# An MLP on one core: TensorE's instructions taken in the order of the program's text instead of the scheduler's

## The chip, the cores and the metric

The kernel runs on one core of a Trainium2 chip. The metric is the device time of one execution in microseconds (us); the median of several executions is compared. Engines are named as in the profile: PE (TensorE, matmuls), PEld (its weight loads), DVE (VectorE), ACT (ScalarE), POOL (GpSimd) and SP (SyncE, which here issues the DMAs).

## What is computed

One transformer block with adaptive layer norm, for 2048 tokens of width 576, in float32. Attention is linear; the MLP has 4608 hidden columns.

```python
mod = (_silu(c) @ w_mod).reshape(c.shape[0], 6, 1, -1)
sa, ca, ga, sb, cb, gb = (mod[:, i] for i in range(6))
h = _layernorm(x) * (1 + ca) + sa
x = x + ga * linear_attention(h, A_wqkv, A_wo)
h = _layernorm(x) * (1 + cb) + sb
x = x + gb * (_silu(h @ B_w1) @ B_w2)
```

## The kernel before

Every float32 product is made of rounded parts: an operand is split into a high part (a cast on ACT) and a low part (a subtraction, on DVE or POOL), and three matmuls (high by high, high by low, low by high) replace one.

The stages before the MLP (modulation, attention, the second layer norm, and the first of 18 groups of hidden columns) end at about 405 us. The change touches what follows: the MLP for groups 1 to 17, each of 256 hidden columns. A group is worked through in two **units**, one per pair of 512-token blocks, so there are 34 units. Both matrix products of the MLP are done by a Winograd scheme with seven products where eight block products would be needed:

- **Up** products (class Unit, `up`, matmuls at L941): seven per unit, taken in the order 1, 6, 2, 5, 7, 3, 4 (ORDER). Each has six matmuls of 128x512; products 2, 3, 4 and 5 have two more for the last 64 of the 576 columns (the tail). They accumulate in three of four PSUM banks named `up`. Between products DVE and ACT take results out: a copy to `p1` (L954), additions into four tiles `f` (L958, L965, L979) and SiLU (L961, L980). f of the first block's second half of columns is complete after product 3.
- **Operands** for the down products are made from the four `f` tiles by `operands1` and `operands2`: sums on POOL (L999 to L1010), casts on ACT (L989) and subtractions on DVE or POOL (L990), into the tiles ha, hd, hb, hc, he, one set for each block of the pair and one buffer for each tile.
- **Down** products (`down`, matmuls at L1029): fourteen per unit, numbered 0 to 13, seven for each block in the order ha, hd, hb, hb, hc, hc, he. Each has six matmuls of 128x288. They alternate between two PSUM buffers named `down`; after each product DVE adds the buffer into an accumulator in SBUF (L1033), and the product after the next one accumulates in the same buffer, so it waits for that addition. A unit's down products are done while the next unit's up products are done.
- **Streams**: ten of the fourteen up operands of a group don't fit in SBUF and are fetched from DRAM (`fetch`, L917), all seven of the first unit and three of the second. There are three rooms: when streamed product i is done, the fetch of product i+3 is issued. A fetch is 1024 KB, or 1280 KB with the tail.
- **Weights** (class Weights): the next group's weights are loaded (L871, L873, L889), summed on POOL (L862 to L865) and split by ACT and DVE (L883, L905, L62) while the present group runs.

In the last group the additions of U (L1047) and the stores of results come on top; after the last unit its first block has seven down products and its second block is done in plain form (`plain_down`, L1066, 48 matmuls).

The order of instructions on each engine is chosen by the scheduler, which works with a timeline of its own and, among instructions that are ready in it, takes the one that stands first in the program's text. Waits between engines are semaphores; each engine takes its instructions in the order chosen. In the text, the main loop (from L1085 on) writes for each of the seven up products of a unit: one down product of the unit before, the up product, one more down product:

```python
for q, n in enumerate(ORDER):
    if before:
        before.down(2 * q)
    unit.up(n)
    if before:
        before.down(2 * q + 1)
```

In the text below, d0 to d13 are down products and u1 to u7 up products by these numbers, a group is the two units of 256 hidden columns, and a unit takes 50 up matmuls and 84 down matmuls.

Of the kernel before, what the change touches and what calls it, by code (L numbers as in the profile page):

```python
# [21 lines left out]
def kernel(ctx: ExitStack, tc, A_x, A_wqkv, A_wo, B_x, B_w1, B_w2, c, w_mod, out):  # L22
# [8 lines left out]
    V, A, G, T = nc.vector, nc.scalar, nc.gpsimd, nc.tensor  # L31
# [16 lines left out]
    NG = F // (G2 * P)  # L48

    def f32(ap):  # L50
        return ap.bitcast(F32)
# [317 lines left out]
    def v_proj(t):  # L369
        ps, vt = ps2(), vx[t % 2]  # L370
        x_passes([(ps[:, 0, :NV0], cut(wkv, D, NV0)),
                  (ps[:, 1, : D - 2 * HG], cut(wkv, D + 2 * HG, D - 2 * HG))], xsel(t))
        for b, j, n, w in ((0, 0, 2, HG), (1, 2, 2, HG), (1, 4, 1, TAIL)):
            off = 2 * HG if j == 4 else 0
            src = ps[:, b, off : off + n * w].rearrange("p (n w) -> p n w", n=n)
            last = A.copy(vt[:, j : j + n, 0, :w], src), sub_hi(vt[:, j : j + n, 1, :w], src, vt[:, j : j + n, 0, :w])
        return last
# [38 lines left out]
    for t in range(NT):  # L416
        tb, i = t // 4, t % 4
        more = tb + 1 < NB
# [18 lines left out]
        before, after = after, v_proj(t)  # L437
# [8 lines left out]
        for _ in range((0, 2, 1, 1)[t] if t < 4 else 1):  # L446
            q = next(qs)
# [42 lines left out]
    for j, kv in enumerate(kvp):  # L490
        n = min(2, NHC - 2 * j)
# [90 lines left out]
    def load_mlp(g):  # L582
        f0 = g * FW
        r1 = rawp.tile([P, KC + 1, FW], F32, name="raw")
        nc.sync.dma_start(r1[:, 0:KC, :], B_w1[0 : KC * P, f0 : f0 + FW].rearrange("(k p) f -> p k f", p=P))
        for h in range(2):
            nc.sync.dma_start(r1[h * 64 : h * 64 + 64, KC, :], B_w1[KC * P : D, f0 : f0 + FW])
        w1 = wg.tile([P, 9, FW], F32R, name="w")
        A.copy(w1[:, 0:KC, :], r1[:, 0:KC, :])
        sub_hi(w1[:, KC : 2 * KC, :], r1[:, 0:KC, :], w1[:, 0:KC, :])  # L590
        wt = rawp.tile([P, 2, FW], F32R, name="wt")
        G.memset(f32(wt[64:128, 1, :]), 0.0)
        tail_w(wt, r1[:, KC, :])
        r2 = rawp.tile([P, KC + 1, FW], F32, name="raw").rearrange("p k f -> p (k f)")[:, : G2 * D]
        r2 = r2.rearrange("p (j d) -> p j d", j=G2)
        nc.sync.dma_start(r2, B_w2[f0 : f0 + FW, :].rearrange("(j p) d -> p j d", p=P))
        w2 = wg.tile([P, G2, 2, D], F32R, name="w")
        V.tensor_mul(r2, r2, bc["gb"].unsqueeze(1).to_broadcast([P, G2, D]))
        A.copy(w2[:, :, 0, :], r2)
        sub_hi(w2[:, :, 1, :], r2, w2[:, :, 0, :])  # L600
        return w1, w2, wt
# [75 lines left out]
    ORDER = (1, 6, 2, 5, 7, 3, 4)  # L677
# [101 lines left out]
    while s < NT + 5 or filler or turns:  # L779
        if s < QB - 2:  # L780
            filler.append(late_q)
        if s == 4:
            w = load_mlp(0)
# [4 lines left out]
        t = s - 2  # L788
# [36 lines left out]
    first = tc.alloc_tile_pool(name="first", bufs=1, reuse_waits="tile")  # L825
# [5 lines left out]
    U = [pf.tile([P, 2, HALF], F32, name=f"U{b}") for b in range(NB)]  # L831
# [80 lines left out]
    def fetch(i):  # L912
        if i < len(streamed):
            _, q, n = streamed[i]
            room = rooms0[i] if i < 2 else rooms[(i - 2) % 3]
            m = hd[q, n].shape[1]
            nc.sync.dma_start(f32(room[:, :m, :]), hd[q, n])  # L917
            in_room[i] = room
# [150 lines left out]
            V.tensor_add(halves(acc[t]), ps[:, :, :HALF], halves(acc[t]))  # L1069
            nc.sync.dma_start(of[t * P : (t + 1) * P, :], acc[t])  # L1070

    w = Weights(1)
    w.load1()
    w.sums1()
    for n in ORDER:
        w.up(n)
    w.load2()
    for i in range(5):
        fetch(i)
    for u in U:  # L1080
        G.memset(u, 0.0)
    ws = {1: w}
    ph, before = None, None
    units = [(g, p) for g in range(1, NG) for p in range(2)]
    for g, p in units:  # L1085
        unit = Unit(g, p, ws[g])
        more = g + 1 < NG
        if p == 1 and more:
            ws[g + 1] = Weights(g + 1)
            ws[g + 1].load1()  # L1090
            ws[g + 1].sums1()
        for q, n in enumerate(ORDER):
            if before:
                before.down(2 * q)
            unit.up(n)
            if before:
                before.down(2 * q + 1)
                if q == 0:
                    before.operands1(1)
                    before.operands2(1)  # L1100
            if p == 0 and q == 1:
                unit.w.sums2()
            if q == 2:
                if ph is None:
                    first.release()
                    ph = tc.alloc_tile_pool(name="ph", bufs=1, reuse_waits="tile")
                unit.operands1(0)
            if q == 5:
                unit.operands2(0)
            if p == 0:  # L1110
                unit.w.down(*{2: (1, 7), 4: (2, 4), 5: (5, 6), 6: (3,)}.get(q, ()))
            if p == 1 and more:
                ws[g + 1].up(n)
        if p == 1 and more:
            ws[g + 1].load2()
        before = unit
    unit.plain_operands(1)
    unit.add_u(3, (1, 1), (1, 0), (0, 1))
    for m in range(7):
        unit.down(m)  # L1120
    for t in range(4):
        unit.plain_down(1, t)
    psC.release()
    for p in (rs, ph, pf, wm, w2p, wqp, hTa, accp):
        p.release()
# [28 lines left out]
```

## Time and profile before

| | us |
|---|---|
| median of three runs | 1275.38 |
| lowest and highest | 1274.17, 1277.03 |
| the profiled execution | 1279.52 |
| its span (first to last instruction) | 1277.7 |
| first up matmul of the changed part | 405.31 |
| last matmul | 1273.64 |

Mean granted clock of TensorE over the span: 0.989.

| line, engine | what | count | busy, us | mean, ns |
|---|---|---|---|---|
| L1033 DVE | `acc` from a down product | 335 | 250.6 | 751 |
| L1033 DVE | `U` from a down product | 134 | 100.8 | 752 |
| L941 PE | up matmul, `hT` operand | 876 | 231.0 | 397 |
| L1029 PE | down matmul, `hc` operand | 804 | 128.2 | 300 |
| L980 ACT | SiLU | 102 | 64.4 | 631 |
| L990 POOL | subtraction for `hc` | 67 | 87.3 | 1303 |

How to read it: the page gives one profiled execution. Matmuls overlap in the pipeline, so a matmul's mean of 397 ns is longer than the step from one start to the next, and a busy share of PE near 1 doesn't mean that matmuls follow each other at full pace; the steps are read from the start times in the timeline. In brackets behind an instruction stand the idle time of its engine before it and what ended it.

### The profile page before, as it was taken

How to read it: one execution, taken by the hardware profiler on the slowest of the kernel's cores; microseconds unless marked ns; L12 is line 12 of the kernel's file. 1: busy time of each engine (PE TensorE's matmuls, PEld its weight loads, DVE VectorE, ACT ScalarE, POOL GpSimd, SP SyncE). 2: the span in 40 equal slices, each digit the busy share in tenths (PEclk: the TensorE clock that was granted, in tenths of full speed). 3: DMA queues.
4: the chain of work that ended last, by engine and by line, in shares of the span. 5: the costliest groups of instructions: out<-in, count | busy, mean ns of one | idle time of the engine just before them, and what ended most of it. 6: DMA issues, size and time to landing. Idle time of an engine off the chain costs nothing.

```text
span 1277.7 us, 19286 instructions
## 1 busy us (share of the span) xinstructions
PE 1190.5 (93%) x7167; PEld 1061.4 (83%) x7167; DVE 958.4 (75%) x1583; ACT 522.3 (41%) x1067; POOL 599.8 (47%) x673
## 2 busy tenths in 40 slices
PE   5999999999898899999999999999999999999997
PEld 4999999899786688888888888888788888888876
DVE  6655744988775688778788777787778777877877
ACT  5434332254553444434344344344344443443430
POOL 3200001322312577667476566665665665665641
PEclk9999999999898999999999999999999999999999
DMA  9221300213527877686576766865766777668623
GB/s 271 82 66 56 108 1 1 86 38 121 208 104 279 336 291 275 240 328 256 224 282 267 287 238 233 335 238 233 298 254 262 266 267 275 247 266 330 230 92 139
DMA packets 57579, 268.59 MB, mean 210 GB/s; under 512 B 5450, under 2 KB 20046, under 8 KB 34446
## 3 DMA queue, kind: packets, MB, share of 16 engines
q1 hardware_dynamic: 57486, 267.36, 55.8%
q8 instruction: 57, 0.93, 0.3%
q14 instruction: 36, 0.29, 0.1%
HBM read 250.56 MB, written 16.78 MB: 209 GB/s over the span
## 4 chain that ended last, share of the span: by engine, by line
PE 53%; DVE 19%; DMA 10%; issue 7%; POOL 7%; ACT 3%; SPq 0%; POOLq 0%; ACTq 0%; DVEq 0%
PE up L941 21%; PE down L1029 15%; PE psK L154 8%; DVE acc L1033 5%; DMA hT<-hd 5%; DVE w L62 4%; PE big L154 4%; DMA raw<-in_B_w_dram 2%; DVE hb L990 2%; PE big L655 1%; PE small L641 1%; DVE f L979 1%; POOL t L862 1%; POOL hc L990 1%; PE kvp L390 1%
## 5 line engine op out<-in xcount | busy, mean ns | idle before, releaser
L1033 DVE TENSOR_TENSOR acc<-down,acc 128x576 f32<-128x576 f32 x335 | 250.6, 751 | 86.7 <-PE down L1029 83.3
L941 PE MATMUL up<-hT,w 128*128 128x512 f32 x876 | 231.0, 397 | 14.0 <-DMA hT<-hd 10.2
L941 PEld LDWEIGHTS up<-hT,w 128*128 128x128 f32 x876 | 157.8, 188 | 47.6 <-ACT p L954 4.6
L1029 PE MATMUL down<-w,hc 128*128 128x288 f32 x804 | 128.2, 300 | 8.2 <-DVE acc L1033 6.9
L1029 PE MATMUL down<-w,hb 128*128 128x288 f32 x804 | 128.8, 300 | 7.2 <-DVE U L1033 4.6
L1029 PEld LDWEIGHTS down<-w,hc 128*128 128x128 f32 x804 | 115.9, 189 | 21.9 <-DVE acc L1033 13.8
L1029 PEld LDWEIGHTS down<-w,hb 128*128 128x128 f32 x804 | 117.5, 191 | 16.9 <-ACT ha L989 3.9
L154 PE MATMUL psK<-w,hT 128*128 128x288 f32 (+2 forms) x896 | 125.3, 297 | 3.0 <-DVE hT L62 1.1
L154 PEld LDWEIGHTS psK<-w,hT 128*128 128x128 f32 x896 | 120.8, 189 | 4.3 <-DVE hT L62 1.9
L1033 DVE TENSOR_TENSOR U<-down,U 128x576 f32<-128x576 f32 x134 | 100.8, 752 | 18.1 <-PE down L1029 16.3
L980 ACT ACTIVATE f<-f 128x512 f32<-128x512 f32 x102 | 64.4, 631 | 116.2 <-DVE f L979 114.3
L990 POOL TENSOR_TENSOR hc<-s,hc 128x512 fp32r<-128x512 f32 x67 | 87.3, 1303 | 31.8 <-ACT hc L989 31.3
L1005 POOL TENSOR_TENSOR s<-f,f 128x256 f32<-128x256 f32 x67 | 54.8, 819 | 94.0 <-ACT f L980 93.3
L941 PE MATMUL up<-room,w 128*128 128x512 f32 x336 | 89.8, 398 | 3.4 <-ACT w L883 2.8
L1010 POOL TENSOR_TENSOR f<-f,s 128x256 f32<-128x256 f32 x67 | 51.8, 773 | 83.2 <-DVE hb L990 81.7
L62 DVE TENSOR_TENSOR w<-raw,w 128x288 fp32r<-128x288 f32 (+2 forms) x139 | 76.3, 557 | 10.2 <-ACT w L883 7.6
L990 POOL TENSOR_TENSOR hd<-s,hd 128x256 fp32r<-128x256 f32 x67 | 54.2, 808 | 50.8 <-ACT hd L989 27.8
L1029 PE MATMUL down<-w,he 128*128 128x288 f32 x402 | 68.4, 305 | 8.4 <-DVE acc L1033 7.8
L941 PEld LDWEIGHTS up<-room,w 128*128 128x128 f32 x336 | 61.4, 190 | 15.6 <-ACT w L883 3.9
L62 DVE TENSOR_TENSOR w<-t,w 128x256 fp32r<-128x256 f32 (+1 forms) x102 | 61.5, 603 | 16.9 <-ACT w L905 12.5
L1029 PEld LDWEIGHTS down<-w,he 128*128 128x128 f32 x402 | 57.2, 188 | 19.7 <-DVE acc L1033 17.6
L1029 PE MATMUL down<-w,ha 128*128 128x288 f32 x402 | 66.1, 300 | 5.3 <-DVE U L1033 4.8
(220 smaller groups left out, 2350.0 us busy)
## 6 DMA issues: line engine op xcount, KB each, us to landing
hT<-hd SPq DMA_DIRECT2D x69, 1280.0 KB, 7.5
hT<-hd SPq DMA_DIRECT2D x43, 1024.0 KB, 6.7
room<-hd SPq DMA_DIRECT2D x33, 1280.0 KB, 7.2
room<-hd SPq DMA_DIRECT2D x23, 1024.0 KB, 6.5
raw<-in_B_w_dram SPq DMA_DIRECT2D x18, 576.0 KB, 6.2
raw<-in_B_w_dram SPq DMA_DIRECT2D x18, 512.0 KB, 5.1
hd<-S SPq DMA_DIRECT2D x6, 1024.0 KB
xt<-in_A_x_dram SPq DMA_DIRECT2D x16, 288.0 KB, 5.2
```

The costliest lines, as they stand in the source:

```text
L62: return V.tensor_sub(lo, full, f32(hi))
L154: T.matmul(ps, xpart(a), wpart(b), start=n == 0, stop=n == len(XW) - 1)
L390: T.matmul(o, vt[:, j, h, :], pkt[:, :, j * HG : j * HG + P], start=(t == 0 and h == 0 and j % 2 == 0), stop=(t == NT - 1 and h == 1), ski ...
L641: T.matmul(ps, left, right, start=n == 0, stop=n == len(seq) - 1)
L655: T.matmul(ps[:, h, :HALF], hs[:, j, a, tok], w2[:, j, b, h * HALF : (h + 1) * HALF], start=n == 0, stop=n == len(seq) - 1)
L941: T.matmul(ps, left, right, start=first and m == 0, stop=m == len(seq) - 1, skip_group_check=True)
L980: A.activation(f, f, AF.Silu)
L990: eng.tensor_sub(t[:, :, 1, :], src, f32(t[:, :, 0, :]))
L1005: G.tensor_add(s[:, 0:1], half(i, 0, 1), half(i, 1, 1))
L1010: G.tensor_sub(s4, s4, s[:, 1:2])
L1029: T.matmul(ps[:, p, :HALF], self.a[i, n][:, u, p * P : (p + 1) * P], self.w.w2[n][:, v], start=n in (1, 5, 7, 6) and j == 0, stop=j == 2, ...
L1033: V.tensor_add(dst, ps[:, :, :HALF], dst)
```

## The change

The whole MLP part, from the first weights of group 1 to the last plain down product, is put into a block in which the order of PE's instructions is that of the text. The other engines' instructions in the block are still ordered by the scheduler, which plans them anew around that order of PE. Nothing else is changed; the body is only indented.

```diff
-    w = Weights(1)
-    w.load1()
-    w.sums1()
...
-    for t in range(4):
-        unit.plain_down(1, t)
+    with tc.manual_schedule(engines={mybir.EngineType.PE}):
+        w = Weights(1)
+        w.load1()
+        w.sums1()
...
+        for g, p in units:
+            unit = Unit(g, p, ws[g])
...
+            for q, n in enumerate(ORDER):
+                if before:
+                    before.down(2 * q)
+                unit.up(n)
+                if before:
+                    before.down(2 * q + 1)
+                    if q == 0:
+                        before.operands1(1)
+                        before.operands2(1)
...
+        unit.plain_operands(1)
+        unit.add_u(3, (1, 1), (1, 0), (0, 1))
+        for m in range(7):
+            unit.down(m)
+        for t in range(4):
+            unit.plain_down(1, t)
```

More of the change, by code (lines that the diff above doesn't have):

```diff
@@ L1070, in plain_down @@
             nc.sync.dma_start(of[t * P : (t + 1) * P, :], acc[t])
-    w = Weights(1)
-    w.load1()
-    w.sums1()
[L1075 to L1111, printed above, removed]
-            if p == 1 and more:
[L1113 to L1120, printed above, removed]
-    for t in range(4):
-        unit.plain_down(1, t)
+    with tc.manual_schedule(engines={mybir.EngineType.PE}):
+        w = Weights(1)
+        w.load1()
+        w.sums1()
+        for n in ORDER:
+            w.up(n)
+        w.load2()
+        for i in range(5):
+            fetch(i)
+        for u in U:
+            G.memset(u, 0.0)
+        ws = {1: w}
+        ph, before = None, None
+        units = [(g, p) for g in range(1, NG) for p in range(2)]
+        for g, p in units:
+            unit = Unit(g, p, ws[g])
+            more = g + 1 < NG
+            if p == 1 and more:
+                ws[g + 1] = Weights(g + 1)
+                ws[g + 1].load1()
+                ws[g + 1].sums1()
+            for q, n in enumerate(ORDER):
[7 more added lines that the diff above has]
+                        before.operands2(1)
+                if p == 0 and q == 1:
+                    unit.w.sums2()
+                if q == 2:
+                    if ph is None:
+                        first.release()
+                        ph = tc.alloc_tile_pool(name="ph", bufs=1, reuse_waits="tile")
+                    unit.operands1(0)
+                if q == 5:
+                    unit.operands2(0)
+                if p == 0:
+                    unit.w.down(*{2: (1, 7), 4: (2, 4), 5: (5, 6), 6: (3,)}.get(q, ()))
+                if p == 1 and more:
+                    ws[g + 1].up(n)
+            if p == 1 and more:
+                ws[g + 1].load2()
+            before = unit
+        unit.plain_operands(1)
[4 more added lines that the diff above has]
+            unit.plain_down(1, t)
```

## The prediction

> **What bounds the kernel now.** I read the page first: busy shares, then the chain that ended last.
>
> ```profile
> PE 1190.5 (93%) x7167; PEld 1061.4 (83%) x7167; DVE 958.4 (75%) x1583; ACT 522.3 (41%) x1067; POOL 599.8 (47%) x673
> PE 53%; DVE 19%; DMA 10%; issue 7%; POOL 7%; ACT 3%; SPq 0%; POOLq 0%; ACTq 0%; DVEq 0%
> ```
>
> TensorE is the bound, but the chain spends a fifth of its time on DVE. The change touches only the MLP, whose first matmul starts at 405.31 us. From the start times in the timeline of PE I take the undisturbed step of one matmul: 0.2317 us in an up product (six take 1.39, eight take 1.85) and 0.1317 us in a down product (six take 0.79). The MLP has 1700, 2814 and 48 (L1066) of them: 393.9 + 370.6 + 6.3 = 771 us. It really takes 405.31 to 1273.64 = 868 us, so **97 us are lost**. Cut by every 100 up matmuls (one group of two units: 45.3 us undisturbed), the loss is 8.9 us to 445, 6.7 to 538, 65.1 in the thirteen groups from 538 to 1192 (mean 5.0, length 50.3), and 16.9 at the end. The timeline of PE shows where a group loses:
>
> ```profile
> 676.62 1.74 PE L1029 MATMUL down<-w,hb 128*128 128x288 f32 x12
> 678.43 2.09 PE L1029 MATMUL down<-w,hc 128*128 128x288 f32 x12
> 681.09 1.06 PE L1029 MATMUL down<-w,he 128*128 128x288 f32 x6 [0.57 <-DVE acc L1033]
> 682.22 1.06 PE L1029 MATMUL down<-w,ha 128*128 128x288 f32 x6
> 683.12 0.95 PE L1029 MATMUL down<-w,hd 128*128 128x288 f32 x6
> 684.22 1.04 PE L1029 MATMUL down<-w,hb 128*128 128x288 f32 x6 [0.15 <-DVE U L1033]
> 685.09 1.54 PE L941 MATMUL up<-S,w 128*128 128x512 f32 x6
> ```
>
> Eight down products in a row take 8.47 us, not 6.32. They alternate between two PSUM buffers, each must be added out by DVE (L1033, 0.751 us) before the next but one may start, and there is no up product to cover that. Sorting all stretches from 538 to 1192 by length: 30 runs of four to eight downs lose 47.8 of the 65 us; 69 single downs lose 5.1, 49 pairs 3.2 (0.06 each), 147 stretches of ups 9.1 (0.06 each). Such a run occurs about once per unit. The windows view, with PE, PEld, DVE, ACT, POOL busy, shows DVE's side:
>
> ```profile
> 788.48:802.54 14.06, 14.06 (x77) 12.22 (x76) 12.52 (x20) 7.20 (x17) 11.37 (x14) 1.00 0.64 238
> 676.62:685.09 8.47, 7.62 (x49) 6.52 (x48) 7.08 (x13) 3.67 (x9) 2.81 (x3) 1.00 0.66 249
> 538.00:1192.00 654.00, 622.36 (x3485) 537.00 (x3485) 509.15 (x807) 270.94 (x586) 405.81 (x468) 1.00 0.70 265
> ```
>
> From 788.48 to 802.54 ups alternate with single downs and pairs; PE loses nothing although DVE is 89% busy.
>
> **The change, part by part.** No instruction is added, removed or resized on any engine; only PE's order is fixed.
>
> *Steady groups.* In the text order a unit is d0 u1 d1, d2 u6 d3, and so on, so between two ups stand two downs, never more. The cover of an eviction: a down's last matmul ends 0.95 us after its start; the next product in its buffer starts 2.97 us after it (0.79 + 0.79 + 1.39) or 3.43 with a tail, so the 0.75 us addition may start up to 1.2 us late at no cost. With pairs at 0.06 and ups at 0.06 a group loses 14 x 0.06 + 14 x 0.06 = 1.7 us, its length is 47.0, the gain 5.0 - 1.7 = 3.3, over thirteen groups **43 us**. DVE's work is 509.15 / 13 = 39.2 us a group, 83% of 47.0, less than the 89% above. Bounds: no loss at all gives 65 us; if DVE in order can't pass its present 78%, 39.2 / 0.78 = 50.3 and the gain is 0.
>
> *The two groups before* (445 to 538) lose 6.7 and would lose 3.4: **3 us**.
>
> *Start.* Now ready later products fill in for missing operands; in strict order they can't. Product 3's fetch is issued at 410.2 as now and lands at 415.6, product 4's about 3.3 later, near 419 (1280 KB at the 400 GB/s of the busiest windows), so the seven ups of the first unit end near 420.8 instead of 416.9: 3.9 lost. The 2.5 us wait at 429.4 (DVE, L1033) and its slow clock need not come: 6 in place of 8.9, **2.5 us** (bounds -3 and +5).
>
> The clock is granted at 1.00 in every 51 us window from 456 to 1221; at 432.93 it goes to 0.5 for 3.41 us, right after those 2.5 us of idle. [...] Product 3's wait (413.2 to 415.6) is as long as the one at 429.4 and could bring the half clock too; 3.41 us at half speed cost 1.7 us, inside the bounds above.
>
> *End.* After the last up 16 downs and 48 matmuls follow now (27.4 us, 18.9 undisturbed), as downs lag behind ups there by a unit; in the text order only 8 downs and the 48 (12.6). DVE's work there is 8 + 4 evictions, 6 additions of U and 3 smaller, about 15 us, and bounds it. I take 9 lost instead of 16.9: **8 us** (bounds 2 and 12).
>
> Sum: 43 + 3 + 2.5 + 8 = 56.5 us off the profiled execution's 1279.5 (span 1277.7), 1223; that execution is 4.1 above the median 1275.4, so in the median's terms 1275.4 x 1223 / 1279.5 = 1219. I take **1222**, leaving 3 us for a chain that is sometimes late.
>
> [...] L62's 128x256 subtractions take 0.41 us in the shortest rows, but 0.547 (w<-raw) and 0.669 (w<-t) on average. All DVE groups with both inputs in SBUF, set at their shortest, have about 33 us in excess, 2.5 a group. [...]
>
> **The rivals.**
>
> *DVE or DMA takes part of it back.* For: DVE is in order; it idles 84.6 us from 538 to 1192 on PE at L1033, behind which other work queues. Ups of a group's first unit then take seven fetches in 22.6 us, 8192 KB, 371 GB/s, against 393 to 411 in the three full 4 us windows from 644 to 656; a fetch is issued when product i is done and is due 7.98 us later (six downs and two ups), with 6.5 to 7.5 median to landing. SP's queue is in order too: the weight load at L889 waited 2.3 us on DVE at 642 and held a fetch behind it. Against: fetches at even steps queue less than today's bunches, and DMA waits are small:
>
> ```profile
> PE down L1029 <- DVE acc L1033: 9.9, 25, 1.2
> PE up L941 <- DMA hT<-hd: 6.1, 7, 1.7
> ```
>
> At 3 to 4.5 us lost per group the gain is 13 x 0.5 to 2 plus about 8: **1240 to 1268**.
>
> *Slower: operands too late, and no filler.* Now ups run about a unit ahead; in the text order product 2's operand (hb of the first half) is due 7.2 us after product 3's last matmul (five downs, u4, u1: 3.95 + 1.85 + 1.39). The chain is add, SiLU, cast, subtraction; in the unit whose product 3 ended at 686.9:
>
> ```profile
> 687.76 0.67 DVE L979 TENSOR_TENSOR f<-up,f 128x512 f32<-128x512 f32 x1
> 690.32 0.63 ACT L980 ACTIVATE f<-f 128x512 f32<-128x512 f32 x1
> 690.98 0.62 ACT L989 CAST hb<-f 128x512 fp32r<-128x512 f32 x1
> 693.50 0.68 DVE L990 TENSOR_TENSOR hb<-f,hb 128x512 fp32r<-128x512 f32 x1
> ```
>
> It ended at 694.18, 7.2 us after: six weight casts went before the SiLU. In the unit after it the same four steps ended 3.0 us after product 3 (713.2 to 716.2). So the chain fits in one kind of unit and just fits in the other, where in the text order the weight casts come one per up, spread over the unit. It turns when the chain exceeds 7.2 by 1.65 us in each unit (2 x 1.65 eats the 3.3). At 10 us it is 2.8 a unit, 5.6 a group: 13 x (5.6 - 3.3) = 30 lost there less 13 gained elsewhere and some more half clock: **1280 to 1315**.
>
> *It doesn't do what it says, or nothing moves.* If the planner's own order comes out, or the other engines' order, planned anew around PE, gives the same waits at other places, it stays at **1273 to 1278**. The runs of downs speak against the first.
>
> **How the numbers follow.** Forecast 1205 to 1240: 0.60. Part taken back, 1240 to 1268: 0.20. No change: 0.05. Slower: 0.15. A change of 0.2% (2.6 us) is about what a measurement of this kernel can tell from none, so faster 0.80, same 0.05, slower 0.15. The range takes in the forecast and the second case and a little below (no loss in the steady groups): 1202 to 1268.
>
> **What would show it.** No run of more than two downs before the last up; a group in about 47 us; eight downs after the last up; waits of PE on L1033 mostly gone; DVE over 80% busy from 538 on. Wrong if PE waits for hb or hc (L989, L990), if waits on DMA hT exceed 20 us, or if the clock falls below 1.00 in mid-stage.

## The result, and the profile after

The changed kernel takes 1218.7 us (median of four, 1214.5 to 1219.4), the kernel before 1276.2 in the same runs; the ratio is 0.953, 95% interval 0.947 to 0.959. The forecast was 1222, in a range of 1202 to 1268.

The page of the changed kernel, first the busy shares, then the chain that ended last:

```profile
span 1217.3 us, 19338 instructions
PE 1158.2 (95%) x7167; PEld 1052.3 (86%) x7167; DVE 979.5 (80%) x1583; ACT 523.9 (43%) x1067; POOL 600.3 (49%) x673
PE 62%; DVE 23%; issue 6%; DMA 5%; ACT 2%; POOL 2%; SPq 0%; DVEq 0%; POOLq 0%; ACTq 0%
```

The counts of each engine's instructions are the same (the total on the first line, 19286 before, also counts those for registers, branches and semaphores). In the chain PE's part grew from 53% to 62% and DVE's from 19% to 23%, while DMA's and POOL's shrank (10% to 5%, 7% to 2%): a part in the chain is not a loss. PE's timeline shows the order of the text, here six of the down products of the kind that stood in one run before (start, duration, engine, line, operation, result and operands):

```profile
1055.77 1.55 PE L941 MATMUL up<-hT,w 128*128 128x512 f32 x6
1057.16 0.98 PE L1029 MATMUL down<-w,hd 128*128 128x288 f32 x6
1058.31 1.03 PE L1029 MATMUL down<-w,hb 128*128 128x288 f32 x6 [0.17 <-DVE U L1033]
1059.18 1.56 PE L941 MATMUL up<-hT,w 128*128 128x512 f32 x6
1060.58 0.95 PE L1029 MATMUL down<-w,hb 128*128 128x288 f32 x6
1061.36 0.95 PE L1029 MATMUL down<-w,hc 128*128 128x288 f32 x6
1062.14 1.52 PE L941 MATMUL up<-room,w 128*128 128x512 f32 x6
1063.51 0.61 PE L941 MATMUL up<-room,wt 128*128 128x512 f32 x2
1063.96 0.95 PE L1029 MATMUL down<-w,hc 128*128 128x288 f32 x6
1064.75 0.95 PE L1029 MATMUL down<-w,he 128*128 128x288 f32 x6
1065.54 1.55 PE L941 MATMUL up<-hT,w 128*128 128x512 f32 x6
```

From 1059.18 on an up product takes 1.39 or 1.40 us from its start to the next one (1.82 with its tail of two matmuls) and each down 0.78 or 0.79, the undisturbed steps: nothing is lost. PE's waits from 500 to 1149 are now only these:

```profile
PE down L1029 <- DVE U L1033: 8.5, 24, 0.6
PE down L1029 <- DVE acc L1033: 2.9, 3, 1.0
```

In the windows view, the thirteen groups that lost 65 us before (columns as in the prediction: us, then PE, PEld, DVE, ACT, POOL busy, clock, DMA share, GB/s):

```profile
540.45:1148.89 608.44, 597.30 (x3487) 530.87 (x3486) 528.58 (x808) 271.16 (x585) 407.21 (x468) 1.00 0.78 285
```

A group takes 608.44 / 13 = 46.8 us instead of 50.3 and loses 1.5 instead of 5.0. By the same count as in the prediction (undisturbed steps against start times):

| part | lost before, us | lost after | gain | forecast |
|---|---|---|---|---|
| start (first 100 up matmuls) | 8.9 | 6.3 | 2.5 | 2.5 |
| two groups | 6.7 | 2.9 | 3.9 | 3 |
| thirteen groups | 65.1 | 19.6 | 45.5 | 43 |
| end | 16.9 | 8.1 | 8.8 | 8 |

Together 60.7 us; the two spans differ by 60.4.

### The profile page after: what moved, and what is told of

It reads as the page before. It is cut to its first block, busy times and chain, and to the rows that moved or that the text cites. A ratio compares the mean times of both kernels' runs of the same rounds, so it can differ in the third digit from the quotient of the medians.

```text
span 1217.3 us, 19338 instructions
## 1 busy us (share of the span) xinstructions
PE 1158.2 (95%) x7167; PEld 1052.3 (86%) x7167; DVE 979.5 (80%) x1583; ACT 523.9 (43%) x1067; POOL 600.3 (49%) x673
## 3 DMA queue, kind: packets, MB, share of 16 engines
q1 hardware_dynamic: 57486, 267.36, 60.4%
## 4 chain that ended last, share of the span: by engine, by line
PE 62%; DVE 23%; issue 6%; DMA 5%; ACT 2%; POOL 2%; SPq 0%; DVEq 0%; POOLq 0%; ACTq 0%
PE down L1029 21%; PE up L941 21%; PE psK L154 10%; DVE w L62 5%; PE big L154 4%; DVE U L1033 3%; DVE acc L1033 3%; DMA raw<-in_B_w_dram 2%; DVE raw L893 2%; DVE hb L990 2%; DVE f L979 1%; DVE ha L990 1%; PE small L641 1%; PE kvp L390 1%; DMA hT<-hd 1%
## 5 line engine op out<-in xcount | busy, mean ns | idle before, releaser
L1033 DVE TENSOR_TENSOR acc<-down,acc 128x576 f32<-128x576 f32 x335 | 245.6, 747 | 17.2 <-PE down L1029 14.2
L941 PE MATMUL up<-hT,w 128*128 128x512 f32 x876 | 227.2, 394 | 4.6 <-DMA hT<-hd 4.6
L1029 PE MATMUL down<-w,hc 128*128 128x288 f32 x804 | 122.8, 295 | 0.6 <-DVE acc L1033 0.6
L989 ACT CAST hc<-s 128x512 fp32r<-128x512 f32 x67 | 41.7, 622 | 135.0 <-POOL s L1007 135.0
L941 PE MATMUL up<-room,w 128*128 128x512 f32 x336 | 86.4, 392 | 0.0
L1007 POOL TENSOR_TENSOR s<-s,f 128x256 f32<-128x256 f32 x67 | 74.4, 1111 | 2.7
L1029 PE MATMUL down<-w,hd 128*128 128x288 f32 x402 | 64.5, 296 | 5.8 <-DVE acc L1033 5.8
L154 PE MATMUL big<-w,qT 128*128 128x288 f32 x448 | 66.1, 301 | 2.1 <-DVE den L510 1.4
L1029 PEld LDWEIGHTS down<-w,hd 128*128 128x128 f32 x402 | 57.3, 188 | 11.6 <-ACT f L980 9.9
L941 PE MATMUL up<-hT,wt 128*128 128x512 f32 x206 | 64.7, 395 | 0.0
```

The costliest lines, as they stand in the source:

```text
L154: T.matmul(ps, xpart(a), wpart(b), start=n == 0, stop=n == len(XW) - 1)
L941: T.matmul(ps, left, right, start=first and m == 0, stop=m == len(seq) - 1, skip_group_check=True)
L989: A.copy(t[:, :, 0, :], src)
L1007: G.tensor_sub(s[:, 1:2], s[:, 0:1], half(i, 0, 0))
L1029: T.matmul(ps[:, p, :HALF], self.a[i, n][:, u, p * P : (p + 1) * P], self.w.w2[n][:, v], start=n in (1, 5, 7, 6) and j == 0, stop=j == 2, ...
L1033: V.tensor_add(dst, ps[:, :, :HALF], dst)
```

## The experiments

**Theory A:** the time was lost in runs of down products, where evictions by DVE (and what stands ahead of them in its queue) have no up product beside them; the text order spaces them and still leaves operands enough time. **Theory B:** the gain came with the order's being fixed at all, that is from the new plan of DVE, ACT and POOL or from evener fetches. A second rival: DVE's total work is the bound, before and after.

**Runs in a fixed order, and evictions made cheaper.** In the loop of the text:

```diff
-                if before:
-                    before.down(2 * q)
+                if before and q == 6:
+                    for m in range(6, 14):
+                        before.down(m)
                 unit.up(n)
                 if before:
-                    before.down(2 * q + 1)
+                    if q < 6:
+                        before.down(q)
```

This kernel is called runs8_full. The down product after the sixth up joins the eight, so its runs are of nine.

> TensorE's order stays fixed, but in each unit the downs are spread otherwise: one after each of the first six ups, then eight in a row ahead of the seventh, as the scheduler's order had it. Theory A (the time was lost in long runs, where evictions by DVE have no up product beside them): 1.2 to 2 us lost per run, so 4 to 5.5 us per group again instead of 1.5, 1255 to 1285 us in all. Theory B (the gain came from DVE, ACT and POOL being planned anew, or from fetches at steadier steps, and any fixed order gives it): 1215 to 1230 us.

In a second kernel with these runs (runs8_half), and in a third with the text order of the change (pairs_half), evictions add half of the columns:

```diff
-            V.tensor_add(dst, ps[:, :, :HALF], dst)
+            V.tensor_add(dst[:, :, : HALF // 2], ps[:, :, : HALF // 2], dst[:, :, : HALF // 2])
```

> The fixed order with runs of eight downs, and every eviction of a down product adds only half of the columns (the other half of the output is left out). Theory A: with evictions of about 0.45 us a run of eight costs next to nothing; the time falls to within 8 us of the same halving with pairs. Theory B, or a cost of long runs that lies in TensorE itself: the distance to the version with pairs stays what it is with whole evictions.

> The changed kernel (pairs of downs), every eviction adding only half of the columns (half of the output left out). Theory A: evictions are already covered, so that only the 1.5 us per group still lost can go: 1195 to 1212 us. If DVE still bounds the pace through its total work, the time falls by more than 30 us.

Measured: 1381.7 us with runs (ratio to before 1.080, 1.077 to 1.083), 1328.1 with runs and halved evictions, 1215.1 with pairs and halved evictions, 3 us above its range (one execution each of the two halved ones). B falls: the order is fixed in all three, and with runs it is slower than the scheduler's. Fetches have a small part in that: from 540 to 1149 of runs8_full PE waits 54.2 us for evictions of down products and 16.1 us for fetches. The distance between runs and pairs is 163 us with whole evictions and 113 with halved ones, so halving the evictions takes away about a third of it. A's number was far too low, and halved evictions did not bring runs near pairs: a run of nine loses 4.0 us (before, runs of four to eight lost 1.6 on average) and 2.0 with halved evictions. DVE's total work as the bound of the changed kernel falls as well: with halved evictions DVE is busy for 34.0 us of a group instead of 40.7, and the whole kernel gains 3.6 us, within the scatter of the changed kernel (1214.5 to 1219.4).

What else is in a run shows in the timeline of DVE in the kernel with whole evictions, during the run that PE does up to 649.48:

```profile
642.51 0.45 DVE L62 TENSOR_TENSOR w<-raw,w 128x288 fp32r<-128x288 f32 x1
642.87 0.75 DVE L1033 TENSOR_TENSOR acc<-down,acc 128x576 f32<-128x576 f32 x1
643.54 1.58 DVE L62 TENSOR_TENSOR w<-t,w 128x288 fp32r<-128x288 f32 x1
645.05 0.74 DVE L1033 TENSOR_TENSOR acc<-down,acc 128x576 f32<-128x576 f32 x1
645.72 0.44 DVE L62 TENSOR_TENSOR w<-raw,w 128x288 fp32r<-128x288 f32 x1
646.08 0.75 DVE L1033 TENSOR_TENSOR acc<-down,acc 128x576 f32<-128x576 f32 x1
646.75 0.45 DVE L62 TENSOR_TENSOR w<-t,w 128x288 fp32r<-128x288 f32 x1
647.12 0.68 DVE L990 TENSOR_TENSOR hb<-f,hb 128x512 fp32r<-128x512 f32 x1
```

Between evictions stand subtractions for the next group's down weights (in every second run also a multiplication of weights, L893, of 1.3 to 1.5 us) and for hb. My reading is that the run's own down products free the weight buffers, which ACT refills, so that this work falls due just then. 5.8 us of DVE work other than evictions falls into such a run, 2.2 into the runs (of six to eight) of the kernel before. Two more kernels, one with runs and one with pairs, test that:

```diff
-            sub_hi(w[:, 1], src, w[:, 0])
+            A.copy(w[:, 1], src)
```

> The kernel of runs8_full (runs that proved to be of nine downs), with the low part of each down weight made by a second cast on ACT instead of the subtraction on DVE (so that the low parts are wrong: this part of the computation is left out). In runs8_full 5.8 us of DVE work other than evictions falls into each run (2.2 in the runs of the kernel before), most of it these subtractions: a down product frees a weight buffer, ACT fills it, DVE's subtraction stands ahead of the next eviction. If that makes these runs twice as dear: a run loses about 2 us instead of 4.0, 6 to 7 us less per group, 1270 to 1300 us. If the evictions alone make them dear: over 1345 us.

> The same replacement in the changed kernel (pairs), for comparison. DVE has 3.6 us less per group. The loss per group, 1.5 us, comes from up weights ahead of an eviction, so it stays within 1 us of that: 1203 to 1222 us by either theory; if DVE's total load bounded the pace, it would fall by more than 30 us.

Measured (one execution each): 1329.2 us with runs, between the two forecasts, and 1211.7 with pairs, as forecast. A run of nine loses 2.5 us instead of 4.0. So subtractions for weights and length of evictions are both in it, and each alone leaves half or more of the loss. The crowded ups between the runs lose too, in waits for fetches and for `f` (14.5 us and 8.8 us from 540 to 1140 here). How much of the whole belongs to which isn't settled further.

**Shorter runs.** Two ups, then four downs (d12 and d13 stand behind the seventh up):

```diff
-                if before:
-                    before.down(2 * q)
                 unit.up(n)
                 if before:
-                    before.down(2 * q + 1)
+                    if q % 2:
+                        for m in range(2 * q - 2, 2 * q + 2):
+                            before.down(m)
+                    if q == 6:
+                        before.down(12)
+                        before.down(13)
```

> The changed kernel with two ups and then four downs in a row, in place of one and two; operands get 3 us more time, the number of instructions is the same. Theory A (a down product beyond the second in a row waits for an eviction, and for what stands ahead of it in DVE's queue): 0.4 to 1 us lost per run of four, six runs per group, 3 to 7 us per group instead of 1.5: 1245 to 1305 us. Rival (only runs of seven and more, or a late operand, cost anything): 1215 to 1228 us.

Measured: 1320.3 us, ratio 1.033 (1.029 to 1.036), above the range. From 540 to 1149 PE waits for evictions and for almost nothing else:

```profile
PE down L1029 <- DVE acc L1033: 47.3, 47, 1.9
PE down L1029 <- DVE U L1033: 5.3, 21, 0.4
PE up L941 <- DMA hT<-hd: 0.3, 1, 0.3
```

A run of four loses 0.74 us on average, as expected; the miss is the pair d12, d13, which has only one up ahead of it after a run of four and loses 1.4 us. My reading is that a pair costs nothing only when DVE has caught up before it.

**The order fixed for half of the groups.**

```diff
-    with tc.manual_schedule(engines={mybir.EngineType.PE}):
+    fixed = tc.manual_schedule(engines={mybir.EngineType.PE})
+    fixed.__enter__()
+    if True:
...
         for g, p in units:
+            if (g, p) == (9, 0):
+                fixed.__exit__(None, None, None)
```

> TensorE's order is fixed up to the end of group 8 and left to the scheduler from group 9 on. If the scheduler makes its runs again whatever state it starts from, groups 9 to 16 lose 5 us each and the end 16: about 1250 us (1243 to 1262). If the runs came only from how the MLP starts (ups ahead of downs by a unit), it stays at the order of the text: 1217 to 1228 us.

Measured: 1253.1 us, ratio 0.981 (0.977 to 0.984). Groups 3 to 7 lose 1.3 us each; from group 9 on it is 1.8, 3.0, 5.3, 5.6, 4.0, 5.1, 5.3, 4.6, and the end 17.5. The runs are back within three groups, though the scheduler here starts from the order of the text, so they don't come from how the MLP starts. PE's timeline in group 11, with eight downs in a row and a wait for a fetch behind them:

```profile
924.04 1.75 PE L1029 MATMUL down<-w,hb 128*128 128x288 f32 x12
925.85 1.85 PE L1029 MATMUL down<-w,hc 128*128 128x288 f32 x12
927.90 1.06 PE L1029 MATMUL down<-w,he 128*128 128x288 f32 x6 [0.20 <-DVE acc L1033]
928.80 0.95 PE L1029 MATMUL down<-w,ha 128*128 128x288 f32 x6
929.81 1.06 PE L1029 MATMUL down<-w,hd 128*128 128x288 f32 x6
930.70 0.95 PE L1029 MATMUL down<-w,hb 128*128 128x288 f32 x6
933.14 1.64 PE L941 MATMUL up<-hT,w 128*128 128x512 f32 x6 [1.48 <-DMA hT<-hd]
```

Why the scheduler's own timeline prefers this isn't in any trace.

**How much room the operands have.** Every down product one or two up products earlier:

```diff
-                if before:
-                    before.down(2 * q)
+                m = 2 * (q + 1)          # 2 * (q + 2) in the second kernel
+                if m < 14:
+                    if before:
+                        before.down(m)
+                else:
+                    unit.down(m - 14)
...
```

The other half of the pair is changed likewise with m + 1, and behind the loop the last unit does only the down products that are left.

> The changed kernel with every down product one up product earlier in TensorE's fixed order (still pairs). An operand has 3.0 us less between its up product and its first use: hb is due 4.2 us after product 3 instead of 7.2, he 10.2 instead of 13.6. Theory A (operands are in time because of the room that the text order leaves; in the changed kernel hb was ready after 3.7 us in the group's first unit and 4.95 in its second, he after 8.0 and 11.4): about 1 us late in one of the two units, 1219 to 1245 us. Rival (operands have room to spare, only evictions count): 1215 to 1222, and no wait of PE on ACT or DVE for hb or he.

> The same, two up products earlier: hb is due 0.8 us after product 3. Theory A: 2.9 and 4.2 us late in the two units, 7.1 per group, sixteen groups: about 1330 us (1290 to 1340). If the scheduler, planning around the new order, brings hb to its shortest (2.6 us, its four instructions), 1.8 us late in each unit: 1275. Rival (operands have room to spare): below 1230.

Measured: 1227.3 us (ratio 0.959, 0.956 to 0.962) and 1372.6 (one execution). PE's waits from 540 to 1149, of the first and of the second:

```profile
PE down L1029 <- DVE hb L990: 6.8, 13, 1.5
PE down L1029 <- DVE acc L1033: 4.5, 13, 0.4
PE down L1029 <- POOL he L990: 3.0, 11, 0.3
```

```profile
PE down L1029 <- DVE hb L990: 38.9, 21, 3.2
PE down L1029 <- ACT hb L989: 33.1, 21, 3.3
```

The operands become late as expected: hb and he a little with one slot less, hb by 3.4 us per unit on average with two (72.0 us over 21 units). The second kernel is above its range in part by the half clock: 129.7 us of its MLP run at a granted clock of 0.5 (the mean over its run is 0.944), where the changed kernel has none between 395 and 1200. At 0.5 a down product of the changed kernel takes 1.61 us (1201.66 to 1203.27) instead of 0.79, and PE is busy for 116 us of the 129.7, so they cost at most 58 us, an estimate. So the text order lies one slot from the edge; the slower rival of the prediction was real and missed by 2.6 to 3.5 us.

**DVE's order fixed as well.**

```diff
-    with tc.manual_schedule(engines={mybir.EngineType.PE}):
+    with tc.manual_schedule(engines={mybir.EngineType.PE, mybir.EngineType.DVE}):
```

> The changed kernel with DVE's order fixed to that of the text too. What PE still loses per group in the changed kernel (1.3 us) is a wait for an eviction that stands behind four weight subtractions in DVE's queue; in the text an eviction stands right behind its down product. If that is all that counts: 1198 to 1212 us. If DVE, 87% busy, then loses more by standing at the head of its queue for casts of ACT (ha and hb: 1.2 to 1.4 us from the up product to the cast, four times per group, and the weights' casts): over 1222, 1225 to 1270 us.

Measured: 1380.3 us, ratio 1.078 (1.073 to 1.082), far above the range, though the cause is of the kind expected. From 540 to 1149, what DVE waits for and what PE waits for most, then DVE's timeline:

```profile
DVE wt L62 <- ACT wt L618: 64.8, 11, 6.7
DVE U L1033 <- PE down L1029: 26.0, 22, 1.9
PE down L1029 <- DVE U L1033: 77.6, 32, 6.2
```

```profile
706.99 0.45 DVE L62 TENSOR_TENSOR w<-raw,w 128x288 fp32r<-128x288 f32 x1
713.17 0.42 DVE L62 TENSOR_TENSOR wt<-raw,wt 64x256 fp32r<-64x256 f32 x1 [5.73 <-ACT wt L618]
713.51 0.74 DVE L1033 TENSOR_TENSOR U<-down,U 128x576 f32<-128x576 f32 x1
```

In the text the up weights' tail stands right behind the issue of their load. DVE stands 5.7 us for it with an eviction behind, and PE behind that. I had counted the casts and overlooked the load. The half clock comes here too, for 112.6 us of the MLP (the mean over the run is 0.952); PE is busy for 86 us of them, so at most 43 of the 162 us by which this kernel is slower than the changed one are the clock's, an estimate.

**What the changed kernel still loses.** DVE's timeline at the group's one steady wait (PE waits for the U eviction until 673.67):

```profile
668.17 1.03 DVE L990 TENSOR_TENSOR ha<-f,ha 128x256 fp32r<-128x256 f32 x1
669.13 0.74 DVE L1033 TENSOR_TENSOR acc<-down,acc 128x576 f32<-128x576 f32 x1
669.79 1.00 DVE L62 TENSOR_TENSOR w<-t,w 128x256 fp32r<-128x256 f32 x1
670.71 1.29 DVE L62 TENSOR_TENSOR w<-raw,w 128x256 fp32r<-128x256 f32 x2
671.93 0.68 DVE L965 TENSOR_TENSOR f<-up,p 128x512 f32<-128x512 f32 x1
672.53 0.41 DVE L62 TENSOR_TENSOR w<-t,w 128x256 fp32r<-128x256 f32 x1
672.86 0.75 DVE L1033 TENSOR_TENSOR U<-down,U 128x576 f32<-128x576 f32 x1
```

Four weight subtractions and an addition into `f` stand ahead of it, one of the subtractions at 1.00 us where 0.41 is its shortest. Two kernels move work to POOL, the first (addu_pool) with the first of these edits, the second (w_pool) with both:

```diff
-                V.tensor_add(self.c(b, i, k), self.c(b, i, k), U[b])
+                G.tensor_add(self.c(b, i, k), self.c(b, i, k), U[b])
```

```diff
-            sub_hi(w[:, 2:4], self.b1[n], w[:, 0:2])
+            (G if n in (6, 5) else V).tensor_sub(w[:, 2:4], self.b1[n], f32(w[:, 0:2]))
```

> The changed kernel with the last group's additions of U (L1047) on POOL instead of DVE. Theory A (in the last 25 us DVE bounds, and these additions stand ahead of evictions in its queue: PE waits 1.8 us behind two of them at 1199): the end loses 5 us instead of 8: 1213 to 1217 us. Rival (POOL, then busy with hc and he, takes over the wait): 1218 to 1222 us.

> As addu_pool, and the low parts of two of a group's seven up weights (products 6 and 5) are subtracted on POOL instead of DVE. Theory A (the 1.3 us that PE still loses per group is a burst of weight subtractions ahead of an eviction): 0.5 to 1 us of it goes in sixteen groups, 1200 to 1210 us. Rival (POOL, 67% busy, makes hc, he and the next f late, or its longer work holds DVE's two-input subtractions up): 1216 us or more.

Measured: 1217.7 us (ratio 0.951, 0.948 to 0.954), not to be told from the change itself, the end still losing 7.4; and 1209.4 us (0.945, 0.943 to 0.947), **the fastest version of the study**. Nine of its fourteen groups after the first two now lose less than 1 us (most 0.45), the others up to 2.2. That the remaining loss came from the burst is borne out in these nine; in each of the other five PE waits 0.7 to 0.9 us for an eviction into `acc` instead. Moving the additions of U alone is not shown to help.

## Why the prediction was right, point by point

- **What bounds the kernel.** Right. Runs of downs cost the time: fixed orders with runs of nine and of four are slower than the scheduler's, and taking the order away again brings runs and loss back. But not all of the 47.8 us that the prediction booked to the runs was theirs: 35.2 lie between a run's downs, and 12.6 between its last down and the up behind it. All of PE's waits for a fetch (6.1 us, 7 times) and for the cast of an up weight (2.8 us, 5 times) from 538 to 1192 stand there. They went with the change as well; whether the runs cause them isn't tested.
- **Steady groups.** Forecast 1.7 us lost per group, measured 1.5. Pairs lose 0.04 each (0.06 taken), and the table of stretches carried over. The row from 788.48 to 802.54, in which DVE is 89% busy and PE loses nothing, had made that likely.
- **DVE's load.** The term was too small. 39.2 us per group became 528.58 / 13 = 40.7, 87% of a group, not 83%. The subtractions for hb and ha are longer, below from 540 to 1149 of the changed kernel, where before they took 708 and 498 ns on average:

```profile
L990 DVE TENSOR_TENSOR hb<-f,hb 128x512 fp32r<-128x512 f32 x53 | 45.3, 854 | 0.0
L990 DVE TENSOR_TENSOR ha<-f,ha 128x256 fp32r<-128x256 f32 x52 | 41.2, 792 | 3.7 <-ACT ha L989 3.1
```

  Beside POOL they are longer on average. In the thirteen groups of the changed kernel an ha subtraction never runs without a POOL instruction beside it (52 of 52, 0.79 us on average; before, 28 of 52); the 24 that ran alone before took 0.42 us at most, and the 26 hb that run alone now 0.68, against 0.99 on average for the 26 beside POOL. Evictions take at most 0.76 us beside POOL or alone. The share of POOL in a group went only from 62 to 67%, but more of these subtractions fall beside its work. The group's loss stayed below the forecast even so.
- **Start.** 6.3 lost, 6 forecast. Products 3 and 4 wait 2.4 and 1.9 us for their fetches, as worked out, and the half clock after product 3 didn't come.
- **End.** 8.1 lost, 9 forecast. Eight downs and the 48 matmuls follow the last up. One wait there is 1.8 us, behind two additions of U, and the clock goes to 0.5 for 3.41 us after it, at 1200.63.
- **Fetches.** The case that evener steps queue less was right: the median from issue to landing of a 1280 KB fetch into `hT` fell from 7.5 to 5.6 us, and PE's waits on fetches from 6.1 us after 538 to none.
- **The slower rival.** Its chain was bounded at 3.0 and 7.2 us; in the changed kernel hb is ready 3.7 and 4.95 us after product 3 in the two units. The margin is 2.6 to 3.5 us, and the kernels with earlier downs show its edge. Its price was too low, as it left out most of the half clock.
- **Planned anew, the other engines give the same waits at other places.** Not so on the whole: PE's waits went but for those on evictions, which fell from 15.2 to 10.9 us in the thirteen groups (those of U alone grew from 5.3 to 8.0).

## What to carry to other kernels

When an engine loses time in one kind of instruction, sort the stretches between the others by length before blaming the engine that it waits for: here the same evictions cost next to nothing in pairs and microseconds in runs, with DVE busy for 89% of the stretch shown with pairs and 84% of the run shown. A fixed order on the bounding engine pays where it spreads such work evenly and its operands have a margin that can be read from the trace; shift it by a slot to learn how much. The same fix, put on DVE as well, which waits for loads and casts, cost 162 us here.

## What was not expected of the hardware

The kernel with downs two slots early had a mean granted clock of 0.93 from 540 to 1149, where the changed kernel had 1.00 from 540.45 to 1148.89. In the former none of PE's waits is above 3.3 us, and those for hb are together 3.4 us per unit on average.

```profile
540.00:1149.00 609.00, 535.53 (x2896) 471.77 (x2895) 439.01 (x669) 231.00 (x486) 331.45 (x389) 0.93 0.64 234
```

In the traces of the two kernels the length of a wait alone doesn't tell whether the clock falls behind it. After a wait of 2.39 us at the start of the changed kernel it stayed at 1.00; after one of 2.52 us in the kernel before it went to 0.5 for 3.41 us, at 432.93, and after one of 1.78 us at the end of the changed kernel it did so too, at 1200.63. In this order:

```profile
416.66 1.64 PE L941 MATMUL up<-hT,w 128*128 128x512 f32 x6 [2.39 <-DMA hT<-hd]
431.93 2.39 PE L1029 MATMUL down<-w,hc 128*128 128x288 f32 x12 [2.52 <-DVE acc L1033]
1199.15 1.04 PE L1029 MATMUL down<-w,hd 128*128 128x288 f32 x6 [1.78 <-DVE acc L1033]
```

What sets the first of the three apart is not shown here.
